# Spreading one batch's dense, transpose, gate and rank pieces over the next batch's score units

## The chip, the cores and the metric

The kernel runs on one core of one Trainium2 chip. The core's engines are TensorE (PE; its weight loads are shown apart, as PEld), VectorE (DVE), ScalarE (ACT), GpSimd (POOL) and SyncE (SP), which here only issues DMAs. Each engine works through its own list of instructions; semaphores hold an instruction back until what it needs is there. The metric is the device time of one launch in microseconds, the median of several runs.

## The reference

Two stages. The first is attention with a selection of key chunks: 4 batches, 8 heads, 768 positions, head size 64. For every query, an upper bound of its score against each 32-key chunk is computed, and the six best causal chunks are kept.

```python
k_min = np.min(k_chunks, axis=3); k_max = np.max(k_chunks, axis=3)
ub = np.sum(np.maximum(q[:, :, :, None, :] * k_min[:, :, None], q[:, :, :, None, :] * k_max[:, :, None]), axis=-1)
ub = np.where(causal, ub, -1e9)
top_chunks = np.argsort(ub, axis=-1)[..., -6:]
...                                   # mask: chunk selected and key not after query
attn = softmax(where(mask, q @ k.T / 8, -1e9));  out = attn @ v
```

The second takes the result as x, 3072 tokens of 512 numbers, through a dense two-layer network and, for each token, one of eight experts of the same form:

```python
y_dense = np.maximum(x @ w1_dense, 0) @ w2_dense
logits = x @ w_gate
expert_idx = np.argmax(logits, axis=1);  gate_w = softmax(logits)[expert_idx]
for e in range(8):
    mask = expert_idx == e
    y_moe[mask] = gate_w[mask, None] * (np.maximum(x[mask] @ w1[e], 0) @ w2[e])
return y_dense + y_moe
```

## The kernel before

Heads are worked in 16 pairs, four pairs to a batch. The scores of a pair are cut into 11 *units*: a unit is up to 512 columns of scores in one PSUM tile, one exponential on ACT, for three of the eleven a diagonal mask on POOL, and then the products with V.

```python
def scores(p, u):
    sp = psc.tile([128, 512], FP, name="sp")            # 3 PSUM buffers
    for g, kt, a, z in units[u]:
        nc.tensor.matmul(sp[:, o : o + w], kT..., rT..., ...)
    ex = aexp.tile([128, 512], HF, name="ex")
    nc.scalar.activation(ex[:, 0:o], sp[:, 0:o], AF.Exp, scale=-0.125)
    if pc[0][1] == pc[0][2]:
        latest["pool"] = nc.gpsimd.affine_select(out=ex, ...)
...
def norm(p, g):                                          # a head's rows into the batch's x tile
    nc.vector.tensor_tensor(xbig[b % 2][:, :, h0 : h0 + D], opv[:, :, 0:D], rs..., ALU.mult)
```

While batch b+1 is in attention, batch b's x goes through the second stage's first steps in small *pieces*: `xtr` (four transposes and a DVE copy), `gate` (24 small matmuls, a chain of small DVE operations), `ranks` (each token's row in a table sorted by expert), `place` (an indirect DMA, issued by POOL, that scatters 128 rows of x into that table in DRAM), and the dense network: `l1` (four matmuls, a relu on ACT) and `l2` (four matmuls, a copy on ACT, a store). In the attention part all of these share one PSUM buffer.

```python
for kind in ("tr", "h", "y", "rk"):
    cur[kind] = (pfill, "fb")                            # pfill: bufs=1
...
def xtr(mi):
    def f():
        tp = ptile("tr", [128, NK, 128], HF, "tp")
        for ko in range(NK):
            nc.tensor.transpose(tp[:, ko], xbig[b % 2][:, mi, ko * 128 : (ko + 1) * 128], ident)
        nc.vector.tensor_copy(xT[:, :, mi * 128 : (mi + 1) * 128], tp)
    return f
def gate():
    lg = ptile("tr", [128, NT, E], FP, "lg")
    ...                                                  # 24 matmuls; max, subtract, Exp, argmax, one-hot
    nc.vector.reciprocal(xbig[b % 2][:, :, Dm : Dm + 2].bitcast(FP), ss)
    nc.gpsimd.tensor_copy(xbig[b % 2][:, :, Dm + 2 : Dm + 4].bitcast(mybir.dt.int32), num[:, b * NT : (b + 1) * NT])
def l2(g, i, hold):
    def f():
        yp = ptile("y", [128, Dm], FP, "yp")
        for j in range(NK):
            nc.tensor.matmul(yp, hold["h"][:, j, i * 128 : (i + 1) * 128], wd[:, NK + j], ...)
        ys = my.tile([128, Dm], FP, name="ys")
        nc.scalar.copy(ys, yp)
        m = b * NT + g * G + i
        for j in range(NJ):
            st_ = nc.sync.dma_start(out=outv[m, j], in_=ys[64 * j : 64 * j + 64])
    return f
```

Which piece comes behind which of the next batch's 44 units is set here (NT is 6, HP*NU is 44):

```python
at = {}
for n, f in enumerate(out_list):                         # six xtr, then gate
    at.setdefault(n + n // NT, []).append(f)
at.setdefault(9, []).append(ranks)
for t in range(NT):
    at.setdefault(11 + 4 * t, []).append(place(t))
U = HP * NU
for n, f in enumerate(dense):                            # 4 l1, 3 l2, 4 l1, 3 l2
    at.setdefault(10 + n * (U - 12) // len(dense), []).append(f)
```

The source order is not the final one: a scheduler in the compiler orders each engine's instructions by readiness and priority. The second part takes the table block by block: `fetch` loads 128 rows of one expert (SyncE, into one of `eg`'s buffers), `tx` transposes them, `e1`, `th`, `e2` are the expert's two layers, and an indirect DMA adds the rows to the output. A fetch may start only when the scatters it could read have landed. The first six fetches are issued in the last pair; the last batch's own pieces go between the first blocks.

## Time and profile before

| | |
|---|---|
| time, median of 3 runs | 259.59 us (258.28 to 259.83) |
| span of the profiled execution | 256.5 us |
| granted TensorE clock over the span | 0.989 |
| HBM read, written | 41.66 MB, 18.23 MB |
| exponentials (L551), busy on ACT | 176, 92.4 us |
| score matmuls (L547), busy on PE | 384, 63.0 us |
| dense matmuls (L383, L392), busy on PE | 128 and 96, 26.2 and 24.4 us |

Line names such as L551 are lines of the kernel. "Busy" is the time in which an engine has an instruction in work; the ends of matmuls are modelled, so the spacing of starts tells more of PE's rate than durations do. "Idle before" is the time for which the engine stood before an instruction, with the one that released it behind an arrow. The page's view of the chain that ended last holds only POOL's final entry in this profile, so limits have to be read from stretches of time and from timelines.

### The profile page before, as it was taken

Reading aid. Unit: us, or ns where it says so; the run is one execution under the profiler, and the core shown is the slowest. Engines: PE = TensorE matmul, PEld = TensorE weight load, DVE = VectorE, ACT = ScalarE, POOL = GpSimd, SP = SyncE. Lnnn points to the kernel's source line nnn. Section 1 sums busy time; section 2 is a strip of 40 time slices with the busy share of each in tenths; the row PEclk is TensorE's granted clock in tenths of the full one; section 3 lists DMA queues with packets and bytes.
Section 4 is the critical chain, followed back from the end, with each engine's and each line's share of the span. In section 5 each row is a group of like instructions: output and inputs, shape, how many; then the busy total and the mean of one; then the engine's idle time right before and its main releaser. Section 6 shows DMA issues by size and latency. Waiting matters only on the chain. (4 is left out here: it accounts for less than half of the span.)

```text
span 256.5 us, 7304 instructions
## 1 busy us (share of the span) xinstructions
PE 213.9 (83%) x2547; PEld 142.2 (55%) x2547; DVE 181.2 (71%) x622; ACT 177.7 (69%) x331; POOL 161.5 (63%) x197
## 2 busy tenths in 40 slices
PE   0379787787899798899996989979999999999960
PEld 0256565575666576656664766646555555555520
DVE  6878899999968699985799997236633345455440
ACT  2689897887679888878897777964556455555430
POOL 3756988766468575867866553520787462888771
PEclk9999999999999999999999999999999999999995
DMA  7999999999749989999999894366398999688875
GB/s 181 263 265 254 209 252 235 247 224 213 199 107 225 252 204 212 202 290 171 279 230 247 140 181 125 87 169 176 98 301 133 242 277 240 113 138 107 112 105 76
DMA packets 75109, 49.89 MB, mean 195 GB/s; under 512 B 29632, under 2 KB 68160, under 8 KB 75072
## 3 DMA queue, kind: packets, MB, share of 16 engines
q1 hardware_dynamic: 59856, 30.33, 46.5%
q0 software_dynamic: 15216, 19.09, 45.4%
q8 instruction: 21, 0.34, 0.6%
q14 instruction: 16, 0.13, 0.1%
HBM read 41.66 MB, written 18.23 MB: 234 GB/s over the span
## 5 line engine op out<-in xcount | busy, mean ns | idle before, releaser
L551 ACT ACTIVATE ex<-sp 128x512 f16<-128x512 f32 (+1 forms) x176 | 92.4, 593 | 10.8 <-PE sp L547 10.6
L547 PE MATMUL sp<-rT,kT 128*128 128x128 f16 (+3 forms) x384 | 63.0, 262 | 2.4 <-ACT ex L551 0.8
L553 POOL TENSOR_SCALAR_AFFINE_SELECT ex<-ex 128x512 f16<-128x512 f16 x48 | 33.2, 699 | 37.6 <-ACT ex L551 37.5
L713 POOL DMA_INDIRECT out_dram<-yo,xg x28 | 43.7, 1561 | 20.2 <-DVE yo L712 12.1
L566 PE MATMUL op<-v,ex 128*128 128x65 f16 x672 | 48.7, 194 | 4.3 <-POOL ex L553 2.8
L566 PEld LDWEIGHTS <-ex 128*128 128x128 f16 x672 | 37.0, 98 | 17.7 <-POOL ex L553 6.2
L712 DVE TENSOR_SCALAR yo<-yp,xg 128x512 f32<-128x512 f32 x28 | 21.0, 750 | 24.9 <-PE yp L709 17.1
L368 POOL DMA_INDIRECT table<-xbig,slot x24 | 24.4, 1019 | 19.1 <-DVE nf L324 11.3
L547 PEld LDWEIGHTS <-kT 128*128 128x128 f16 x384 | 28.3, 98 | 6.7 <-issue 4.2
L703 ACT COPY ehT<-tp 128x512 f16<-128x512 f16 x28 | 16.4, 585 | 19.8 <-PE tp L701 19.8
L692 PE MATMUL hp<-we,exT 128*128 x112 | 29.1, 379 | 1.1 <-DVE xbig L577 1.1
L709 PE MATMUL yp<-we,ehT 128*128 x112 | 28.7, 379 | 0.8 <-ACT ehT L703 0.8
L383 PE MATMUL hp<-xT,wd 128*128 128x384 f16 x128 | 26.2, 325 | 1.7 <-ACT hT L385 1.1
L392 PE MATMUL yp<-wd,hT 128*128 128x512 f16 x96 | 24.4, 378 | 1.0 <-ACT ys L395 0.4
L695 ACT ACTIVATE eh<-hp 128x512 f16<-128x512 f32 x28 | 16.7, 598 | 11.5 <-PE hp L692 10.9
L395 ACT COPY ys<-yp 128x512 f32<-128x512 f32 x24 | 14.2, 593 | 10.2 <-PE yp L392 6.6
L490 DVE TENSOR_TENSOR k<-kp 128x384 f16<-128x384 f16 x32 | 13.8, 469 | 9.9 <-ACT kp L483 9.8
L385 ACT ACTIVATE hT<-hp 128x384 f16<-128x384 f32 x32 | 15.9, 496 | 6.6 <-PE hp L383 6.3
L686 DVE COPY exT<-tp 128x512 f16<-128x512 f16 x28 | 11.8, 423 | 11.5 <-PE tp L684 10.5
L483 ACT COPY kp<-pp 128x768 f16<-128x768 f16 x16 | 12.9, 804 | 7.9 <-PE pp L481 7.9
L577 DVE TENSOR_TENSOR xbig<-op,rs 128x384 f16<-128x384 f32 x32 | 17.6, 550 | 0.4
L475 POOL CAST v<-vf 128x768 f16<-128x768 f32 x16 | 13.9, 871 | 5.0 <-DMA vf<-in_v_dram 3.0
(124 smaller groups left out, 403.0 us busy)
## 6 DMA issues: line engine op xcount, KB each, us to landing
we<-in_moe_w_dram POOLq DMA_DIRECT2D x16, 512.0 KB, 8.2
kf<-in_k_dram SPq DMA_DIRECT2D x32, 192.0 KB
qf<-in_q_dram SPq DMA_DIRECT2D x32, 192.0 KB
vf<-in_v_dram SPq DMA_DIRECT2D x32, 192.0 KB
out_dram<-ys SPq DMA_DIRECT2D x48, 128.0 KB
xg<-table SPq DMA_DIRECT2D x28, 136.0 KB
table<-zt SPq DMA_DIRECT2D x9, 136.0 KB
wd<-in_moe_w_dense_dram POOLq DMA_DIRECT2D x2, 512.0 KB, 6.3
```

The source lines that it names most:

```text
L368: sc = nc.gpsimd.indirect_dma_start(out=table, out_offset=bass.IndirectOffsetOnAxis(ap=keep["slot"][:, t : t + 1], axis=0), in_=xbig[b % 2 ...
L383: nc.tensor.matmul(hp, wd[:, ko, j * 128 : (j + 1) * 128], xT[:, ko, g * G * 128 : (g + 1) * G * 128], start=(ko == 0), stop=(ko == NK - 1))
L392: nc.tensor.matmul(yp, hold["h"][:, j, i * 128 : (i + 1) * 128], wd[:, NK + j], start=(j == 0), stop=(j == NK - 1))
L547: nc.tensor.matmul(sp[:, o : o + w], kT[p % NB][g][:, kt * 128 : (kt + 1) * 128], rT[p % NB][g][:, a * 128 : z * 128], start=(o == 0), sto ...
L551: nc.scalar.activation(ex[:, 0:o], sp[:, 0:o], AF.Exp, scale=-0.125)
L553: latest["pool"] = nc.gpsimd.affine_select(out=ex, in_=ex, compare_op=ALU.is_ge, fill=0.0, base=0, pattern=[[0, 4], [1, 2], [2, 64]], chan ...
L566: nc.tensor.matmul(s["op", g][:, t * (D + 1) : (t + 1) * (D + 1)], ex[:, o : o + 128], v16[p % NB][:, g, kt, :], start=first, stop=(last_o ...
L577: nc.vector.tensor_tensor(xbig[b % 2][:, :, h0 : h0 + D], opv[:, :, 0:D], rs.to_broadcast([128, NT, D]), ALU.mult)
L692: nc.tensor.matmul(hp, s["xT"][:, ko], wef[:, bass.ds(offs[i] + ko * 512, 512)], start=(ko == 0), stop=(ko == NK - 1))
L709: nc.tensor.matmul(yp, s["hT"][:, j], wef[:, bass.ds(offs[i] + (NK + j) * 512, 512)], start=(j == 0), stop=(j == NK - 1))
L712: nc.vector.tensor_scalar(o, yp, s["x"][:, Dm : Dm + 2].bitcast(FP), None, ALU.mult)
L713: sc = nc.gpsimd.indirect_dma_start(out=out, out_offset=bass.IndirectOffsetOnAxis(ap=s["x"][:, Dm + 2 : Dm + 4].bitcast(mybir.dt.int32), a ...
```

## The change

Pieces are issued one in every two units over all of the next batch's 44 units, in one fixed order: three transposes, a dense piece, a transpose, a dense piece, two transposes, gate, ranks, and the other dense pieces. This is to keep pieces from standing close together on the shared PSUM buffer, and to keep dense matmuls from piling up late in the batch. Scatters follow the ranks three units apart. As pieces of a batch now last longer, a third x tile lets attention write ahead, and the row numbers are written into the tiles by index instructions instead of being copied after the gate. A dense piece's store is issued two units behind the piece, so that SyncE doesn't stand before it with loads behind. To make room, fetch buffers go from 14 to 12 and two key-reduction tiles from two buffers to one. The first fetches move later, since the scatters do.

```diff
-    eg = ctx.enter_context(tc.tile_pool(name="eg", bufs=14))
+    eg = ctx.enter_context(tc.tile_pool(name="eg", bufs=12))
...
-    xbig = [const.tile([128, NT, XW], HF, name=f"xbig{i}") for i in range(2)]
+    NX = 3
+    xbig = [const.tile([128, NT, XW], HF, name=f"xbig{i}") for i in range(NX)]
+    def numbers(b):
+        for j in range(NJ):
+            nc.gpsimd.iota(xbig[b % NX][64 * j : 64 * j + 64, :, Dm + 2 : Dm + 4].bitcast(mybir.dt.int32)[:, :, 0],
+                           pattern=[[128, NT]], base=b * S + j, channel_multiplier=2)
...                                    # called once for each tile at the start
-            nc.gpsimd.tensor_copy(xbig[b % 2][:, :, Dm + 2 : Dm + 4].bitcast(mybir.dt.int32), num[:, b * NT : (b + 1) * NT])
+            if b >= NX:
+                numbers(b)
...
+                hold["ys", i] = ys
+            return f
+        def store(g, i, hold):
+            def f():
+                ys = hold["ys", i]     # then the two DMAs as before
...
-        for n, f in enumerate(out_list):
-            at.setdefault(n + n // NT, []).append(f)
-        at.setdefault(9, []).append(ranks)
+        x, d = out_list[:NT], dense
+        order = x[:3] + [d[0], x[3], d[1], x[4], x[5], gate, ranks] + d[2:]
+        for n, f in enumerate(order):
+            at.setdefault(2 * n, []).append(f)
+            if f in stores:
+                at.setdefault(min(2 * n + 2, HP * NU - 2), []).append(stores[f])
         for t in range(NT):
-            at.setdefault(11 + 4 * t, []).append(place(t))
-        U = HP * NU
-        for n, f in enumerate(dense):
-            at.setdefault(10 + n * (U - 12) // len(dense), []).append(f)
+            at.setdefault(2 * order.index(ranks) + 3 + 3 * t, []).append(place(t))
...
-            k1 = ahead.tile([128, 2, NC, 16], HF, name="k1")
-            k2 = ahead.tile([128, 2, NC, 8], HF, name="k2")
+            k1 = ahead.tile([128, 2, NC, 16], HF, name="k1", bufs=1)
+            k2 = ahead.tile([128, 2, NC, 8], HF, name="k2", bufs=1)
...
-            if p == NP - 2 and u == 8:
+            if p == NP - 2 and u == NU - 1:
                 load_rows(N1)
                 load_offs()
-            if p == NP - 1 and 3 <= u < 3 + FIRST:
-                fetch(u - 3)
+            if p == NP - 1 and 4 <= u < 4 + FIRST:
+                fetch(u - 4)
...                                    # in the second part:
             extra.setdefault(1 + n * (N1 - 2) // len(d), []).append(f)
+            if f in stores:
+                extra.setdefault(2 + n * (N1 - 2) // len(d), []).append(stores[f])
```

## Prediction

> **What bounds the kernel now.** I read the table of engines first, then stretches of time, then TensorE's and the queues' timelines. Over the whole span nothing is full:
>
> ```profile
> PE 213.9 (83%) x2547; PEld 142.2 (55%) x2547; DVE 181.2 (71%) x622; ACT 177.7 (69%) x331; POOL 161.5 (63%) x197
> ```
>
> The span has two parts. Attention lasts until about 171 us: sixteen head pairs of eleven score units, whose 176 exponentials on ACT run from 16.6 to 170.7. The experts' blocks follow. I cut attention at every eleventh exponential and asked for each engine's busy time (columns: stretch, length, then PE, PEld, DVE, ACT, POOL busy, clock, DMA share, GB/s). Pairs 3, 5, 6, 7, 8, 9, 10, 13 and 14, counted from 0:
>
> ```profile
> 40.50:48.70 8.20, 6.54 (x113) 5.15 (x112) 7.95 (x32) 7.00 (x13) 5.97 (x10) 1.00 1.20 248
> ...
> 56.70:69.50 12.80, 9.96 (x156) 7.40 (x155) 12.19 (x50) 9.38 (x18) 7.30 (x9) 1.00 1.01 229
> 69.50:81.10 11.60, 10.79 (x147) 7.50 (x145) 8.72 (x31) 9.65 (x20) 8.32 (x10) 1.00 0.63 121
> 81.10:91.90 10.80, 9.13 (x117) 6.07 (x114) 8.68 (x30) 9.39 (x20) 6.43 (x9) 1.00 1.11 265
> 91.90:99.80 7.90, 6.71 (x121) 5.46 (x118) 7.63 (x28) 6.84 (x14) 5.36 (x7) 1.00 0.90 166
> 99.80:110.50 10.70, 10.02 (x161) 7.47 (x158) 10.41 (x43) 8.50 (x18) 7.16 (x9) 1.00 1.11 241
> 110.50:122.40 11.90, 10.75 (x145) 7.38 (x144) 8.58 (x33) 9.57 (x21) 9.13 (x11) 1.00 1.04 226
> ...
> 141.70:152.50 10.80, 9.54 (x160) 7.27 (x157) 10.52 (x51) 8.54 (x17) 6.35 (x8) 1.00 0.98 173
> 152.50:163.00 10.50, 10.14 (x117) 6.37 (x114) 7.16 (x33) 8.29 (x19) 4.99 (x6) 1.00 0.39 103
> ```
>
> A pair without pieces of the previous batch takes 8.2 us and DVE is busy for 7.95: DVE paces it. With pieces the limit changes hands: in pairs 5, 9 and 13 (transposes, gate, ranks) DVE holds 12.19 of 12.80, 10.41 of 10.70, 10.52 of 10.80; in 6, 10 and 14 (most of the dense pieces) PE holds 10.79 of 11.60, 10.75 of 11.90, 10.14 of 10.50, with DVE far lower. The loads are large in turn instead of together. That is what the change attacks.
>
> Where one limit hands over to the other, PE's timeline shows the pieces standing in its way:
>
> ```profile
> 61.93 0.74 PE L265 MATMUL lg<-wg,xT 128*128 128x8 f16 x24
> ...
> 64.64 0.20 PE L290 MATMUL rk<-oh,low 128*128 128x48 f16 x1 [1.19 <-DVE oh L278]
> ...
> 65.48 0.81 PE L383 MATMUL hp<-xT,wd 128*128 128x384 f16 x4
> 66.13 0.33 PE L534 MATMUL pp<-ident,fl 128*128 128x128 f16 x3
> ```
>
> The rank matmul waits 1.19 us for the gate's chain of small DVE operations, and everything behind it on PE waits too. A first-layer piece (four matmuls) holds PE from 65.48 to 66.13, 0.65 us: durations shown are longer than the spacing, so I count spacings. From 170.7 on PE alone is the limit: busy 57.54 of 58.00 us between 182 and 240, a block about every 2.2 us.
>
> The hand-over between the parts goes through DRAM. Three views, POOL's, SyncE's and PE's timelines:
>
> ```profile
> 164.48 0.97 POOL L368 DMA_INDIRECT table<-xbig,slot  x1 [0.17 <-issue]
> ```
> ```profile
> 166.94 1.44 SPq L450 DMA_DIRECT2D xg<-table  x3
> ```
> ```profile
> 171.33 0.61 PE L684 MATMUL tp<-ident,xg 128*128 128x128 f16 x8
> 173.05 1.02 PE L692 MATMUL hp<-we,exT 128*128 x4 [1.12 <-DVE xbig L577]
> ```
>
> The last scatter of batch 2 into the table starts at 164.48; the first fetch of a block, which must wait for its landing, starts 2.46 us later; its rows are read at 171.33, directly after the last attention matmul, without a wait. So there are some two microseconds to spare.
>
> **What the Trainium skill says.** "Perfetto Trace Analysis", section "Optimization Strategy", says that where the most-contended engine changes over time, interleaving the regimes may help. The stretches above are this case. "PSUM — Partial Sum Buffer", section "Engine vs sequencer instructions", says that matmuls start and complete in program order and the queues of ScalarE, VectorE and GpSimdE are strictly first in, first out; the 1.19 us wait at 64.64, with nothing of PE started in it, agrees. "TensorE: Matmul & The Clock Gate", section "Back-to-back issue gap", gives N/2.4 + 2.5 ns for one warm matmul, 162.5 ns at N=384; the trace has 0.65/4 = 162 ns. "DMA: Bandwidth & Descriptors", section "Two DMAs through the same engine are not ordered", says only a completion semaphore orders a write and a later read; hence the 2.46 us above.
>
> **The change part by part.**
>
> Work per batch stays the same. From spacings: eight first-layer pieces 8 x 0.65 = 5.2 us of PE, six second-layer ones (71.04 to 71.90) 6 x 0.86 = 5.2, six transposes at 0.22 = 1.3, gate 0.6, ranks 0.4: 12.7 us. On DVE six copies of 0.414 = 2.5, gate and ranks about 1.9 more (62.71 to 65.6, without what lies between). On ACT 14 evictions spaced some 0.4 to 0.5, about 6.2.
>
> *Spacing.* Before, six transposes come in units 0 to 5, gate in 7, ranks in 9, dense pieces from 10 to 39. After, transposes, two dense pieces, gate and ranks fill units 0 to 18 and dense pieces go to 42. In the compiled order of PE's instructions I added up what stands between score matmuls, by spacing (0.0285 us for a 65-column one, 0.056 for a transpose): the heaviest pair of each batch carries 10.0, 9.7, 9.8 us before and 7.2, 7.0, 6.0 after; adding 2.24 us of scores (5376 columns at 2.4 per ns) gives 12.2 against 9.4. The longest run without a score matmul falls from 3.5, 2.3, 3.3 to 3.5, 1.6, 1.25: batch 0 keeps its bunch.
>
> After, by units: 0 to 10 are paced by DVE, 7.7 (mean of pairs 1 to 4) + 4 x 0.42 = 9.4. Units 11 to 21 too: 7.7 + 0.8 + 1.9 = 10.4. Then ACT decides, with 6.75 of its own (eleven exponentials at the spacing of 0.485 and two copies of 0.7): 6.75 + 6 pieces x 0.44 = 9.4, and 6.75 + 5 x 0.44 = 9.0. Sum 38.2 a batch. The same sum before, largest engine of each pair: 12.2 + 10.8 + 9.4 + 7.6 = 40.0 in batch 0, and 10.4 + 10.75 + 9.0 + 9.3 = 39.5 in batch 1. All pairs from 56.7 on sum to 106.8 in 114.0 us, so a microsecond of limit costs 1.07. Gain 1.8 + 1.3 in the first two, times 1.07 = 3.3. In batch 2 the last two pairs prepare no further head, so work put off to them was cheap already, and the lists of blocks (about 2.5 us of DVE) now fall a pair later: I count 0.4. Together 3.7.
>
> *Waits of the pieces.* All pieces share one PSUM buffer. PE idle just before transposes is 3.2 us and before ranks 2.1 us between 48.7 and 170.7. A piece two units later finds the buffer free and the gate done. Some of this is already in the 6% above the sum of limits; I count a quarter of the 5.3: 1.3.
>
> *Third x tile, row numbers.* The copy of the row numbers after the gate once held POOL for 2.5 us until scatters had landed; index writes made once replace it. POOL is not the limit there: 0. Four more index writes of 0.15 to 0.36 us at 35.6 lie on a POOL that is 80% busy: 0. The single buffers for the key reduction are written and read by DVE alone: 0.
>
> *Stores queued behind.* SyncE waits 21 us for evictions in attention, and loads stand behind; but POOL's waits for k, q and v in pieces' time are nil. Worth 0.
>
> *Hand-over.* Scatters of batch 2 move from units 11 to 31 to units 21 to 36, so the last stands behind pair 15's last diagonal mask. That mask ends at 168.62 in the old time base: scatter 168.8, landed and first fetch 171.2, data about 1.9 us after that (its packets in the old trace end at 168.5 to 169.2) = 173.1, second block 173.6. The old reads were at 171.33 and the matmul at 173.05 after a DVE wait that will be over by then. New first expert matmul about 174.2: +1.2 lost. One dense piece of 0.86 us now lies in that hole, already counted in the work.
>
> *Expert part.* The 28 blocks are the same; 12 fetch buffers instead of 14 make fetch i wait for scatter i-12. Fetch 12 ran at 197.3, scatter 0 at 182.5 with 5.1 to land: free. The last dense stores come a block later in the source, but in SyncE's compiled order stand behind the same scatter 7: 0.
>
> Sum: -3.7 - 1.3 + 1.2 = -3.8, so 259.6 - 3.8 = 255.8 us.
>
> **Rivals.** *Hand-over dominates.* If attention gets no faster and the late scatter costs 2.5 us: 262. For it: the landing chain is serial and PE reads in order; against it: that attention has idle on every engine. *DVE stays the limit.* DVE's total is unchanged, 92 us of 114 from 56.7 on; it was busy 95% in pairs without pieces, and if the old overload was already absorbed by preparing two pairs ahead, evening out gives nothing: about 259 to 260. *Full evening-out.* DVE and ACT each total some 93; if they are kept 88% busy, attention shrinks by 8 and with the lost 1.2 the time is 253. For it: the three gaps of 4.5 to 5.4 us between exponentials that end at 69.5, 110.5 and 152.5; against it: batch 0 keeps its bunch, and three engines loaded alike wait for each other more.
>
> **Range and chances.** Between the rivals' 253 and 262, with a little beyond: 251.5 to 260.8. Faster by over 2% means below 254.4, that is 5.2 us against the 3.8 worked out: 0.32. Slower by over 2% is above 264.8 and needs more than the whole hand-over loss: 0.05. The rest, 0.63, is within.
>
> **What would show it.** Right: in stretches of eleven exponentials no pair above about 11 us from pair 5 on, DVE no longer over 11 in one; PE's idle before transposes and ranks below 1.5 us together; the last exponential about 5 us earlier; scatter-to-fetch chain ending after attention with PE idle 1 to 2 us before its first block transpose; expert part as long as before. Wrong: the last exponential at the old place, the hole at the hand-over above 3 us, or PE idle in the expert part from late fetches.

## The result, and the profile after

The changed kernel takes 266.26 us (median of 4 runs, 265.66 to 266.54) against 259.33 for the kernel before on the same chip: a ratio of 1.027 [1.023 to 1.031]. It is slower, by almost twice as much as the prediction said it would be faster. The page of the kernel after begins:

```profile
PE 216.7 (82%) x2547; PEld 143.0 (54%) x2547; DVE 186.5 (71%) x622; ACT 178.4 (68%) x331; POOL 161.5 (61%) x200
```

PE and DVE run exactly as many instructions as before and are busy longer: PE by 2.8 us, DVE by 5.3. POOL has three instructions more and the same busy time.

To see where the time went I cut both traces at the same events: every eleventh exponential, the first transposes of the third block (the first of a block that nothing holds up), and the end. "Hand-over" is from the last exponential to that third block, "experts" the rest.

| us | to pair 1 | pairs 1–4 | pairs 5–8 | pairs 9–12 | pairs 13–15 | hand-over | experts | span |
|---|---|---|---|---|---|---|---|---|
| before | 24.3 | 32.4 | 43.2 | 41.8 | 29.0 | 7.5 | 78.3 | 256.5 |
| after | 23.9 | 36.0 | 41.1 | 42.4 | 29.4 | 9.9 | 81.7 | 264.3 |
| difference | -0.4 | **+3.6** | -2.1 | +0.6 | +0.4 | **+2.4** | **+3.4** | +7.8 |

The profiled execution of before is its fastest one (258.28), so the differences sum to 0.9 more than the medians do. Three stages lose. Of the 3.6 us in pairs 1 to 4, pairs 1 to 3 lose 2.1 us (26.5 after, 24.4 before). Pair 4 loses 1.5 (9.43 us; 7.95 before), but there the cut itself moves: after, ACT makes the next pair's q tile ahead of the first exponential of pair 5, before it made it behind. The kernel with the new spacing alone, further below, has 9.37 us in pair 4 as well. So pair 4 belongs to the spacing, and pairs 4 to 8 together take 50.6 us instead of 51.1: batch 0 gains about 0.6 us and not 2.1.

*Pairs with pieces.* Busy time in stretches of the kernel after, for pairs 6, 7, 10 and 11 (columns as in the prediction):

```profile
68.90:80.00 11.10, 10.08 (x153) 7.12 (x150) 9.43 (x40) 8.84 (x20) 8.18 (x10) 1.00 0.74 173
80.00:92.00 12.00, 10.86 (x136) 7.35 (x135) 9.49 (x35) 9.96 (x21) 8.51 (x10) 1.00 0.99 237
...
110.70:123.40 12.70, 11.03 (x156) 7.43 (x156) 11.55 (x41) 9.54 (x20) 9.34 (x11) 1.00 1.03 199
123.40:135.40 12.00, 10.36 (x139) 7.17 (x139) 10.16 (x36) 9.47 (x20) 9.35 (x11) 1.00 1.03 257
```

Pairs 5 and 9 are shorter, as intended (9.0 and 9.6 us; 12.9 and 10.7 before), but the load moved into the two pairs behind each. Counted by the matmuls in PE's timeline, the 14 dense pieces of batch 0 lie about 2, 4, 7 and 1 in pairs 5 to 8 (8, 17, 27 and 4 matmuls), where the prediction counted 2, 1, 6 and 5: even spacing in the source did not come out even. In the stretch from 110.70, PE holds 11.03 us and DVE 11.55 of 12.70: both are near their limit. In the waits of PE between 48.7 and 170.7 us (waits in total, how many, the longest) the pieces' own waits went away, and others came:

```profile
PE pp L533 <- DVE kb L507: 4.7, 5, 1.2
PE sp L560 <- ACT ex L564: 2.5, 6, 0.7
...
PE rk L295 <- DVE oh L282: 1.3, 2, 0.7
...
PE tp L261 <- DVE xbig L590: 0.3, 1, 0.3
```

The same view of the kernel before had:

```profile
PE tp L257 <- DVE xT L258: 2.7, 3, 1.0
PE rk L290 <- DVE oh L278: 2.1, 3, 1.2
...
PE pp L520 <- DVE kb L494: 0.7, 2, 0.5
```

Transposes no longer wait for the copies that free their buffer; ranks still wait 1.3 us. But PE now stands 4.7 us before the chunk scores until DVE has the reduced keys (kb), against 0.7, and 2.5 us before scores until an exponential has freed a buffer.

*Pairs 1 to 4.* Why are the reduced keys late? DVE's timeline after shows the two halving steps of the key reduction (max and min of two halves; x2 is both of them):

```profile
39.21 1.75 DVE L503 TENSOR_TENSOR k<-kp 128x384 f16<-128x384 f16 x2
40.88 2.44 DVE L504 TENSOR_TENSOR k<-k 128x192 f16<-128x192 f16 x2
```

The same two lines before, at nearly the same place:

```profile
40.62 0.65 DVE L490 TENSOR_TENSOR k<-kp 128x384 f16<-128x384 f16 x2
41.19 0.88 DVE L491 TENSOR_TENSOR k<-k 128x192 f16<-128x192 f16 x2
```

1.53 us became 4.19. The work of these lines is the same; what differs is POOL's timeline at that time, here after:

```profile
39.78 0.96 POOL L481 CAST k<-kf 128x768 f16<-128x768 f32 x1
40.69 0.95 POOL L483 CAST q<-qf 128x768 f16<-128x768 f32 x1
41.60 0.66 POOL L566 TENSOR_SCALAR_AFFINE_SELECT ex<-ex 128x512 f16<-128x512 f16 x1
42.22 0.81 POOL L488 CAST v<-vf 128x768 f16<-128x768 f32 x1
```

The four POOL instructions stand without a gap from 39.78 to 43.03, and the second step gets through only about when they end; its first half takes 2271 ns, where the shortest of the 32 takes 243 ns. POOL's set-up block in pair 2 (tiles filled, constants, row numbers) takes 3.8 us instead of 2.7: three tile fills and six index writes instead of two fills and two index writes. So, counted from the start of pair 1, the k cast comes 1.1 us later than before. The key reduction comes 1.05 us earlier, as a DVE copy ahead of it takes 0.39 us instead of 1.45, which before lay beside two masks on POOL. Before, the casts ran from 39.03 to 40.79 and were all but over when the key reduction began. Over the whole kernel the 32 first steps take 582 ns in the mean instead of 469, or 3.6 us more in sum, and the second steps 452 instead of 405, or 1.5 more: nearly all that DVE's busy time grew by.

The Trainium skill, "SBUF — State Buffer", section "SBUF: two separate sides", describes this: VectorE and GpSimd share one pair of SBUF ports as an exclusive lock, taken by a VectorE operation in a two-port mode or, against a GpSimd operation that reads SBUF, by one with two SBUF inputs; the loser "fully blocks". The trace agrees: the step that took 2271 ns has two SBUF inputs and lies under casts and a mask that read SBUF. The prediction did not use it.

*Hand-over.* The last scatter (POOL), the first fetch (SyncE's queue), the first read and the first expert matmul (PE) of the kernel after:

```profile
171.30 0.98 POOL L373 DMA_INDIRECT table<-xbig,slot  x1 [0.17 <-issue]
```
```profile
173.80 3.38 SPq L463 DMA_DIRECT2D xg<-table  x6
```
```profile
176.06 0.40 PE L700 MATMUL tp<-ident,xg 128*128 128x128 f16 x4 [0.94 <-DMA xg<-table]
...
177.50 0.81 PE L708 MATMUL hp<-we,exT 128*128 x3 [0.46 <-DVE exT L702]
```

The chain of scatter, landing, fetch and read is the same as before, but begins only 1.4 us ahead of the last exponential (172.7) instead of 6.2. From the last exponential to the first expert matmul it is now 4.8 us, before 2.4.

*Experts.* From the tenth to the eleventh block after takes 6.5 us, before 3.9. ACT's copies of dense results into store buffers show it, after:

```profile
208.10 0.59 ACT L400 COPY ys<-yp 128x512 f32<-128x512 f32 x1 [2.25 <-DMA out_dram<-ys]
210.40 0.59 ACT L400 COPY ys<-yp 128x512 f32<-128x512 f32 x1 [1.72 <-DMA out_dram<-ys]
```

They wait for earlier stores to land, since there are three such buffers, and PE's second expert layer waits 1.63 us for ACT at 208.74.

In SyncE's queue the stores of dense results that wait there went out ahead of the next two fetches before, and go out behind two (from 200.88) after. Before, then after:

```profile
195.32 1.12 SPq L398 DMA_DIRECT2D out_dram<-ys  x2
```
```profile
201.95 1.12 SPq L409 DMA_DIRECT2D out_dram<-ys  x2
```

Counted from the tenth block (200.5 and 205.0), the store begins 5.2 us ahead of it before, and 3.1 after.

### The profile page after: what moved, and what is told of

Its sections match the earlier page's. It is cut to its first block, busy times and chain, and to the rows that moved or that the text cites. A ratio compares the mean times of both kernels' runs of the same rounds, so it can differ in the third digit from the quotient of the medians.

```text
span 264.3 us, 7322 instructions
## 1 busy us (share of the span) xinstructions
PE 216.7 (82%) x2547; PEld 143.0 (54%) x2547; DVE 186.5 (71%) x622; ACT 178.4 (68%) x331; POOL 161.5 (61%) x200
## 5 line engine op out<-in xcount | busy, mean ns | idle before, releaser
L560 PE MATMUL sp<-rT,kT 128*128 128x128 f16 (+3 forms) x384 | 65.4, 265 | 4.0 <-ACT ex L564 2.9
L579 PE MATMUL op<-v,ex 128*128 128x65 f16 x672 | 49.3, 195 | 3.2 <-POOL ex L566 2.1
L579 PEld LDWEIGHTS <-ex 128*128 128x128 f16 x672 | 37.7, 99 | 15.8 <-POOL ex L566 6.0
L373 POOL DMA_INDIRECT table<-xbig,slot x24 | 24.3, 1012 | 20.2 <-DVE nf L329 12.5
L560 PEld LDWEIGHTS <-kT 128*128 128x128 f16 x384 | 29.1, 99 | 9.2 <-issue 6.3
L388 PE MATMUL hp<-xT,wd 128*128 128x384 f16 x128 | 26.2, 325 | 0.8 <-ACT ys L400 0.3
L397 PE MATMUL yp<-wd,hT 128*128 128x512 f16 x96 | 24.3, 378 | 1.6 <-ACT ys L400 1.0
L711 ACT ACTIVATE eh<-hp 128x512 f16<-128x512 f32 x28 | 16.7, 597 | 11.3 <-PE hp L708 11.3
L503 DVE TENSOR_TENSOR k<-kp 128x384 f16<-128x384 f16 x32 | 17.3, 582 | 7.3 <-ACT kp L496 7.3
L400 ACT COPY ys<-yp 128x512 f32<-128x512 f32 x24 | 14.3, 596 | 11.5 <-PE yp L397 6.3
L533 PE MATMUL pp<-kb,qp 128*128 128x48 f16 x192 | 11.1, 185 | 11.3 <-DVE kb L507 11.2
```

Of the source, the lines that this page charges most:

```text
L373: sc = nc.gpsimd.indirect_dma_start(out=table, out_offset=bass.IndirectOffsetOnAxis(ap=keep["slot"][:, t : t + 1], axis=0), in_=xbig[b % N ...
L388: nc.tensor.matmul(hp, wd[:, ko, j * 128 : (j + 1) * 128], xT[:, ko, g * G * 128 : (g + 1) * G * 128], start=(ko == 0), stop=(ko == NK - 1))
L560: nc.tensor.matmul(sp[:, o : o + w], kT[p % NB][g][:, kt * 128 : (kt + 1) * 128], rT[p % NB][g][:, a * 128 : z * 128], start=(o == 0), sto ...
L579: nc.tensor.matmul(s["op", g][:, t * (D + 1) : (t + 1) * (D + 1)], ex[:, o : o + 128], v16[p % NB][:, g, kt, :], start=first, stop=(last_o ...
```

## The experiments

Each ratio is to the kernel before in the same session on the same chip. The kernel before itself took 258.2 to 264.3 us in six sessions on different chips, so absolute times are compared only within a chip. The stages are from one profiled execution of each.

### One part of the change undone

Stores issued with their pieces again, in the expert part, where it matters:

```diff
-                extra.setdefault(2 + n * (N1 - 2) // len(d), []).append(stores[f])
+                extra.setdefault(1 + n * (N1 - 2) // len(d), []).append(stores[f])
```

> The changed kernel with one edit: in the expert part the last batch's dense stores are issued with their piece again, not one block later. SyncE's order changes in 8 rows, no other engine's order changes. Ledger theory: between the 9th and 15th block transposes the changed kernel lost 3.2 us against the kernel before because its three store buffers were freed late (ACT's copies stood 2.25, 1.72 and 0.90 us for stores to land); so 266.3 - 3 = 263.3 us, with ACT's wait for stores down to about 2 us. Rival: the expert part was late only because it started late, and PE would have stalled on scatters anyway: no change, 265.5 to 266.5.

Row numbers made once and copied after the gate, as before, with three tiles (two long index writes and three copies in pair 2, instead of six index writes):

```diff
-            numbers(b)
...
+        for j in range(NJ):
+            nc.gpsimd.iota(num[64 * j : 64 * j + 64, :, 0], pattern=[[128, NM]], base=j, channel_multiplier=2)
...
-            if b >= NX:
-                numbers(b)
+            nc.gpsimd.tensor_copy(xbig[b % NX][:, :, Dm + 2 : Dm + 4].bitcast(mybir.dt.int32), num[:, b * NT : (b + 1) * NT])
```

> The changed kernel with one edit: row numbers again written once into a table of their own and copied by POOL after the gate, as in the kernel before. Only POOL's order changes. Theory of collisions: POOL's longer block of set-up instructions in pair 2 moved its k and q casts by 0.75 us under DVE's two fp16 key-reduction lines, which then took 1.2 and 2.1 us too long in pair 3; pairs 2 to 4 should go back from 9.1, 9.7, 9.4 to about 8.5, 8.2, 8.0 us and the time to about 263.3. Rival: the single buffers of the key reduction (kept here) make DVE slower: pairs 2 to 4 stay above 9 and the time at 266.

Scatters two units apart instead of three, fetches one unit earlier:

```diff
-            at.setdefault(2 * order.index(ranks) + 3 + 3 * t, []).append(place(t))
+            at.setdefault(2 * order.index(ranks) + 2 + 2 * t, []).append(place(t))
...
-            if p == NP - 1 and 4 <= u < 4 + FIRST:
-                fetch(u - 4)
+            if p == NP - 1 and 3 <= u < 3 + FIRST:
+                fetch(u - 3)
```

> The changed kernel with one edit: the six scatters of a batch follow the ranks two units apart, from unit 20 to unit 30, instead of three apart from 21 to 36, and the first six fetches one unit earlier, so that the last scatter stands where it did in the kernel before. Theory: PE's first block transpose waits for the chain last scatter, landing, fetch, landing (171.3, 173.8, 176.1); with the scatters back it comes within 1 us of the last exponential instead of 3.4, and the time is 266.3 - 2.4 = 263.9. Rival: the fetches stand behind dense stores on SyncE's queue, which haven't moved, so the gap stays above 2.5 us and the time above 265.5.

And all three together:

> The three edits together: what is left of the change is the new spacing of pieces, the third x tile, the fewer buffers and stores two units behind in attention. If the three losses are separate and add up: 266.3 - 3 - 3 - 2.4 = 257.9 us, a little under the kernel before (259.3). Rival, that the spacing itself costs time and the three are symptoms: above 260.

| | ratio to before | pairs 1–4 | pairs 5–8 | pairs 9–12 | hand-over | experts |
|---|---|---|---|---|---|---|
| stores at once | 1.0129 [1.0053, 1.0204] | 35.9 | 41.8 | 42.6 | 10.1 | 80.4 |
| numbers copied | 1.0104 [1.0031, 1.0176] | 34.4 | 41.9 | 42.5 | 9.9 | 81.6 |
| scatters earlier | 1.0077 [1.0051, 1.0104] | 34.0 | 42.9 | 42.3 | 8.3 | 80.8 |
| all three | 1.0051 [1.0026, 1.0076] | 34.3 | 41.7 | 42.3 | 8.3 | 81.0 |

Each ratio is lower than the changed kernel's, which was 1.027 above and is 1.021 in the repeat below. But the changed kernel was not run on this chip, and the first two intervals overlap the repeat's, 1.0123 to 1.0301; only the last two lie clear below it. Nor can the experts column be set against the first table: two kernels further below, whose expert part is that of the kernel before, take 82.3 and 82.5 us there on their chips. All three edits together leave half a per cent of loss. Earlier scatters bring the hand-over from 9.9 to 8.3 us, as they should; but 2.0 us of what this kernel shows is not theirs. It lies in pairs 1 to 4, where no scatter is due and where the compiled order of PE, DVE, ACT and POOL is that of the changed kernel. DVE's second halving step and the mask on POOL, in this run:

```profile
41.05 1.04 DVE L504 TENSOR_TENSOR k<-k 128x192 f16<-128x192 f16 x2
```
```profile
41.87 0.74 POOL L566 TENSOR_SCALAR_AFFINE_SELECT ex<-ex 128x512 f16<-128x512 f16 x1
```

The q cast ends at 41.81 and the mask, whose exponential is some 0.2 us later here, starts at 41.87: in that gap DVE gets in, and the step takes 1.04 us instead of 2.44. In the changed kernel the mask followed the cast without a gap. Pairs 5 to 8, 1.8 us longer here, give most of it back. How often either happens in the timed runs isn't known, so the ratio of this kernel is not to be read to the last tenth, and the 1.6 us that copied numbers win in the same pairs can't be told from it. What the three undone leave is the spacing together with the third tile and its fill, fewer buffers, and the late stores in attention. Pairs 1 to 4 are still 1.9 us longer than in the kernel before, and there is no gain.

### A repeat, and the casts moved

The changed kernel once more on another chip, then both kernels, and the three undone, with the k and q casts issued three units later:

```diff
-            if u == 7:
+            if u == 10:
                 with tc.issue_after(latest["pool"].ins):
                     cast_qk(p + 3)
```

> The changed kernel itself, so that the next ones have it on the same chip. Expected 1.027 of the kernel before, as measured first; the single-edit runs so far (1.013, 1.010, 1.008 on another chip, where the kernel before took 263.3) cannot be read without it.

> The changed kernel with POOL's k and q casts (and the loads behind them) asked for three units later in a pair, at unit 10 instead of 7, so that they no longer run beside DVE's fp16 key reduction. The same work. Collision theory: DVE's SBUF-to-SBUF fp16 lines take 21.2 us longer in sum than their shortest form in the changed kernel, 17.0 in the kernel before; here under 13, the key-reduction lines near 0.31 and 0.21 us, attention 4 us shorter than in the changed kernel on the same chip. Rival: DVE is busy but not what pairs wait for, or the stretch comes back under other POOL work: attention within 1 us of the changed kernel's.

> The kernel before with the same move of the casts. Collision theory: its 17.0 us of stretch fall too, to about 11, and it gets 2 to 3 us faster (ratio about 0.99). Rival: no difference, because the kernel before already had its casts beside other DVE work in most pairs (ratio 1.00), or slower where casts come too late for the transposes.

> The changed kernel with scatters earlier, stores at once in the expert part, row numbers copied, and the casts moved. If the losses of the change are collisions, the hand-over and the late stores, nothing but the spacing is left, and it should beat the kernel before: ratio 0.98 to 0.99. Rival: spacing itself gains nothing: ratio 1.00 or above, no better than the kernel before with moved casts.

The repeat gave 1.0212 [1.0123, 1.0301], with 35.9 us in pairs 1 to 4, 9.7 in the hand-over and 80.3 in the experts: attention and the hand-over come out alike on both chips, the experts 1.4 us apart. Later casts made no version faster: after 1.031 [1.0225, 1.0396], before 1.0126 [1.0034, 1.0218], the three undone 1.0112 [1.0084, 1.014]. In the changed kernel the two key-reduction steps do get shorter, 427 and 342 ns in the mean against 544 and 471 in the repeat. But the casts then stretch other DVE lines: a copy of the queries takes 623 ns instead of 465, one of the keys 510 instead of 399. Pair 1 takes 10.11 us, 7.76 without the move. At this place the collision was moved, not shed; other places were not tried. (The expectations put the undisturbed steps at 0.31 and 0.21 us; the shortest in the traces are 0.34 and 0.24.)

### The collision by itself

To the kernel before, five index writes of a spare tile that nobody reads, in the set-up block:

```diff
+    spare = const.tile([128, 6], mybir.dt.int32)
...
+        for _ in range(5):
+            nc.gpsimd.iota(spare, pattern=[[1, 6]], base=0, channel_multiplier=2)
```

> The kernel before with five idle index writes of POOL added to its set-up block in pair 2 (about 0.75 us of POOL's time, read by nobody); no other engine's order changes. If the changed kernel lost its 3.6 us between pairs 1 and 5 because POOL's casts and masks slid under DVE's fp16 lines, the same slide alone should do it here: pairs 2 to 4 from 8.5, 8.2, 8.0 to above 9 in one or two of them, attention and total 1.5 to 3.5 us longer (ratio 1.006 to 1.013). Rival: POOL has slack there (80% busy) and 0.75 us vanishes: ratio 1.00, pairs as before.

It gave 1.0107 [1.0061, 1.0152]: 0.7 us of idle work on POOL costs some 2.8 us of the kernel. Pairs 1 to 4 take 34.7 us instead of 32.4, and DVE's timeline shows where:

```profile
39.10 3.60 DVE L493 TENSOR_TENSOR k<-kp 128x384 f16<-128x384 f16 x2
```

The line took 0.65 in the kernel before. Counted from the start of pair 1, POOL's casts start 0.6 us later than there, but DVE, whose copy of 1.45 us takes 0.36 here, arrives 1.0 us earlier, and stands under POOL's casts, copies and mask in a row. So a small shift can turn one collision into a worse one.

The second experiment takes one of the two SBUF inputs of the first step away: it reads one half of the keys from PSUM, where the transposes left them. This pairs keys of different chunks, so these three kernels compute other chunk maxima than the reference and choose other chunks; the amount of work stays.

```diff
-                nc.vector.tensor_tensor(k1[:, i], kc[:, :, 0:16], kc[:, :, 16:32], op)
+                nc.vector.tensor_tensor(k1[:, i].rearrange("d (T c) w -> d T c w", c=4),
+                                        pk.rearrange("d (T j c w) -> d T j c w", j=NJ, c=4, w=16)[:, :, 0],
+                                        kp.rearrange("d (T c w j) -> d T c w j", j=NJ, c=4, w=16)[:, :, :, :, 1], op)
```

> The changed kernel with the first key-reduction line reading one of its two operands from PSUM instead of SBUF, the pairs of keys chosen accordingly; same result, same count of instructions, the compiler's order shifts somewhat. Collision theory: these lines took from 0.31 to 1.8 us, 18.6 us in sum; reading PSUM they should all take the same, about 0.45 us, 14.5 in sum, whatever POOL does; attention 2 to 4 us shorter than in the changed kernel. Rival: they stretch as before (then POOL's work is not what stretches them), or they don't and attention is no shorter.

> The kernel before with the same line read from PSUM. It loses 5.0 us of stretch in these lines but each is 0.14 us longer, 4.5 us in sum: no gain expected, ratio 0.995 to 1.005, where the changed kernel gains. Rival: gain as large as in the changed kernel, so that collisions do not tell the two apart.

> The changed kernel with earlier scatters, stores at once and copied row numbers, and the key line read from PSUM: collisions on that line, the hand-over and the late stores are all gone. If these made up the loss: ratio 0.985 to 0.995. If the spacing is worth nothing even so: 1.00.

Ratios: after 1.0291 [1.0227, 1.0356], before 1.0167 [1.0103, 1.0231], the three undone 1.0251 [1.0207, 1.0296]. DVE's groups by shape, in the kernel before with this edit (count, busy us, mean ns):

```profile
L490 DVE TENSOR_TENSOR k<-pp,kp 128x384 f16<-128x384 f16 x32 | 16.6, 550 | 9.3 <-ACT kp L483 9.2
L493 DVE TENSOR_TENSOR k<-k 128x192 f16<-128x192 f16 x32 | 16.3, 538 | 0.0
```

and in the kernel before itself:

```profile
L490 DVE TENSOR_TENSOR k<-kp 128x384 f16<-128x384 f16 x32 | 13.8, 469 | 9.9 <-ACT kp L483 9.8
L491 DVE TENSOR_TENSOR k<-k 128x192 f16<-128x192 f16 x32 | 11.8, 405 | 0.0
```

With a PSUM operand all 32 instances take 535 to 558 ns, whatever POOL does; with both operands in SBUF they took 335 to 997 ns before and 339 to 1795 after. So on this line the stretch goes with the second SBUF input, which fits the condition in the skill's section. As a remedy it fails: the two-SBUF form takes 335 ns at its shortest, and the step behind it, which still reads SBUF twice, now collects the stretch (405 to 538 ns in the mean). So does a copy of the queries in pair 1, 2.22 us instead of 0.75, and that pair takes 11.3 us instead of 7.8.

### One part alone, on the kernel before

The kernel before against itself, as a measure of the comparison:

> The kernel before itself, to have its profile on the chip of the next three: ratio 1.00; pairs 1 to 4 in 32.4 us, pairs 5 to 8 in 43.2, 9 to 12 in 41.8, from pair 13 to the last exponential 29.0, from there to the third block transpose 7.5.

0.9998 [0.997, 1.0026]. The stores one step later than their pieces:

```diff
                 dense.append(l2(g, i, hold))
+                stores[dense[-1]] = store(g, i, hold)
...
             extra.setdefault(1 + n * (N1 - 2) // len(d), []).append(f)
+            if f in stores:
+                extra.setdefault(2 + n * (N1 - 2) // len(d), []).append(stores[f])
```

> The kernel before with one part of the change alone: in the expert part the dense stores come one block later. SyncE's order differs in 8 rows, nothing else. Theory: late stores free the three store buffers late, ACT and then PE stand; the stretch from the third block transpose to the end grows by 2 to 3 us over the kernel before on the same chip, ratio 1.008 to 1.012. Rival: the stall in the changed kernel needs its fewer fetch buffers (12 for 14), which aren't in here: no change.

1.0024 [1.0002, 1.0046]. Its profiled execution has 81.0 us in the experts, against 77.8 in the repeat of before, 5.9 us between the tenth and the eleventh block, and the same wait for a store to land, 1.75 us on ACT. But this execution took 260.71 us, and the median is 259.34 (258.40 to 261.05), so the trace shows the effect at its largest. Alone it is worth 0.6 us in the median. Nor do late stores always cost these blocks time: with scatters earlier, or numbers copied, the stores are as late as in the changed kernel, and from the tenth to the eleventh block it is 3.9 and 4.35 us.

The scatters later, so that the last falls into unit 36 as in the changed kernel, but with the two x tiles of before:

```diff
-            at.setdefault(11 + 4 * t, []).append(place(t))
+            at.setdefault(11 + 5 * t, []).append(place(t))
...
-            if p == NP - 1 and 3 <= u < 3 + FIRST:
-                fetch(u - 3)
+            if p == NP - 1 and 4 <= u < 4 + FIRST:
+                fetch(u - 4)
```

> The kernel before with the scatters five units apart, so that the last one stands at unit 36 as in the changed kernel, and the first fetches one unit later. Theory: the chain scatter, landing, fetch, landing ends after attention; from the last exponential to the third block transpose 9.5 to 10 us instead of 7.5, ratio 1.006 to 1.01. Rival: hidden behind the last batch's own start: below 8 us, ratio 1.00.

1.034 [1.0306, 1.0373], far beyond what was expected. The hand-over takes 11.5 us instead of 7.5, with pairs 13 to 15 as long as before (29.0). The rest lies in two pairs: pair 8 takes 11.25 us instead of 7.97 and pair 12 13.96 instead of 9.56. POOL's timeline gives the cause:

```profile
94.63 0.19 POOL L282 COPY xbig<-num 128x6 int32<-128x6 int32 x1 [4.06 <-DMA table<-xbig,slot]
...
140.19 0.19 POOL L282 COPY xbig<-num 128x6 int32<-128x6 int32 x1 [6.06 <-DMA table<-xbig,slot]
```

and PE's what it costs:

```profile
141.05 0.40 PE L566 MATMUL op<-v,ex 128*128 128x65 f16 x4 [4.67 <-POOL ex L553]
```

With two tiles batch 2 writes into the tile of batch 0, so the copy of its row numbers must wait until the last scatter of batch 0 has read it, and the compiler has put that copy only a few instructions behind the scatter; POOL stands in order behind that copy, the next mask comes late, and PE waits 2.67 us for it in pair 8 and 4.67 in pair 12. The changed kernel, with three tiles, has as late scatters and not this loss: there one index write, that of batch 3, waits 3.0 us, at 94.23, and PE waits for no mask beside it. No run changes the number of tiles alone.

Only the new order and spacing of the pieces, with scatters two units apart, without the third tile, the index writes or the late stores:

```diff
-        for n, f in enumerate(out_list):
-            at.setdefault(n + n // NT, []).append(f)
-        at.setdefault(9, []).append(ranks)
+        x, d = out_list[:NT], dense
+        order = x[:3] + [d[0], x[3], d[1], x[4], x[5], out_list[NT], ranks] + d[2:]
+        for n, f in enumerate(order):
+            at.setdefault(2 * n, []).append(f)
...
-            at.setdefault(11 + 4 * t, []).append(place(t))
+            at.setdefault(2 * order.index(ranks) + 2 + 2 * t, []).append(place(t))
...
```

> The kernel before with the new order and spacing of pieces alone: two x tiles, 14 fetch buffers, stores at once, copied row numbers, two buffers each in the key reduction, last scatter at unit 30. If even loads are worth what the prediction said: pairs 5 to the last exponential 3 to 4 us shorter than in the kernel before, ratio 0.985. What the runs so far suggest: pairs 5 to 8 about 1.5 us shorter, pairs 9 to 12 and the rest up to 1 us longer, 0 to 1 us in all, ratio 0.995 to 1.003.

1.0004 [0.9979, 1.0029]: nothing. Against the repeat of before, pairs 5 to 8 take 41.2 us instead of 43.2, but pair 4 takes 9.37 instead of 8.34, and pairs 9 to 12 take 43.8 instead of 41.8. What batch 0 gains, batch 1 gives back, mainly in pairs 10 and 11, which are 12.78 and 11.91 us long here as in the changed kernel (11.87 and 9.76 before). The profiled execution took 261.37 us, the longest of twelve with a median of 258.93, so its stages sum to 2.4 us too much.

### The set-up block out of the way

At the start POOL waits 2.66 us for the first keys. The last pair of runs puts the whole set-up block there, in both kernels; only the filler store to the table stays in pair 2:

```diff
+        route_consts()
         cast_qk(0)
...
                     with tc.issue_after(st[n2]["cast"].ins):
-                        route_consts()
+                        nc.sync.dma_start(out=table[EMPTY : EMPTY + 128], in_=zt)
```

> The kernel before with its block of set-up work on GpSimd (tiles filled, row numbers, constants) moved out of pair 2 into the 2.66 us in which GpSimd waits for the first keys; the filler store to the table stays where it is. If GpSimd's work as such only costs where it lies beside VectorE's copies and key reductions, pair 2 and pair 3 lose nothing and may gain up to 1 us (the fold's copy of 1450 ns at 37.9 goes back to 362): ratio 0.995 to 1.0. The rival, that every shift of GpSimd's casts only moves the stretch to other lines: VectorE's sum in pairs 1 to 4 as large as before, ratio 1.0 within its interval. A third: the first fills delay the first casts or share VectorE's port during its own fills, and the start grows by up to 1 us: ratio 1.004.

> The changed kernel with the same block (now with three fills and six index writes) in the wait for the first keys. If what pairs 1 to 4 lose against the kernel before (36.0 against 32.4 us) comes from the longer block in pair 2 and the phase of the casts that it sets, the stretch falls to 32 to 33.5 us, the key reductions at 39 to 41 us take 0.4 to 0.9 us instead of 1.75 to 2.44, and the ratio to before falls from 1.021-1.027 to 1.008-1.015 (the late scatters and stores stay). The rival, that the spacing of the pieces or the single key-reduction buffers cost those pairs: they stay above 35 us, ratio 1.02 or more.

| us | to pair 1 | pair 1 | pairs 2–4 | pairs 9–12 | ratio to before |
|---|---|---|---|---|---|
| before | 24.3 | 7.8 | 24.6 | 41.8 | 1 |
| before, block early | 24.5 | 7.8 | 23.8 | 43.8 | 1.0032 [0.9996, 1.0069] |
| after | 23.9 | 7.8 | 28.2 | 42.4 | 1.021 to 1.027 |
| after, block early | 26.2 | 9.7 | 24.8 | 42.5 | 1.0225 [1.0179, 1.0271] |

In the changed kernel pairs 2 to 4 fall from 28.2 to 24.8 us, the level of the kernel before. DVE's timeline has the fourth and the fifth key reduction; the fifth is the one that took 4.19 us:

```profile
34.54 1.28 DVE L502 TENSOR_TENSOR k<-kp 128x384 f16<-128x384 f16 x2
35.74 1.04 DVE L503 TENSOR_TENSOR k<-k 128x192 f16<-128x192 f16 x2
...
43.91 0.63 DVE L502 TENSOR_TENSOR k<-kp 128x384 f16<-128x384 f16 x2
44.46 0.88 DVE L503 TENSOR_TENSOR k<-k 128x192 f16<-128x192 f16 x2
```

The fifth takes 1.51 us in place of 4.19. That settles the cause in these pairs: the block, not the single buffers of the key reduction, which this kernel still has. But pairs 1 to 4 take 34.5 us where 32 to 33.5 were expected, and the total hardly moves. The longer block ends after the first keys have come, so the first cast begins at 6.00 us, the first key reduction stands under casts (2.67 us for its first step at 8.56), and the first exponential comes at 18.1 us instead of 16.3. In pair 1 POOL stands 2.5 us before a weight load, for a cause that the profile doesn't show; its masks come late, PE waits 1.4 us for one, and the casts now lie over the fourth key reduction, which takes 2.32 us instead of 1.50. The start and pair 1 lose somewhat more than pairs 2 to 4 gain. In the kernel before, 0.8 us won in pairs 2 to 4 comes back as a longer pair 10 (13.25 us against 11.86). No version ran faster than the kernel before beyond its interval.

## Why the prediction was wrong

**The bounds and the limits of single pairs** were read rightly: pairs 5, 9 and 13 were DVE's, the dense ones PE's.

**Spacing, predicted 3.7 us gained: measured nothing when alone. This is the largest miss.** For batch 0 the sum of limits seems to hold: pairs 5 to 8 were to shrink by 1.9 us and shrank by 2.1 in the changed kernel. That is luck. Pair 5 came out at 9.0 us and pair 7 at 12.0, where the prediction's limits times 1.07 give 10.1 for both, and with pair 4 the gain is 0.6. For batch 1 it was to be 1.4 and was a loss of 0.6. (The largest engines from 56.7 us on sum to 107.8, not 106.8, and the factor is 1.06; the gain of 3.3 stays.) The step that failed is the sum of "the largest engine of each pair" times 1.07. It gave the units from 22 to 32, which fall mainly into pairs 7 and 11, to ACT with 9.4 us; these pairs took 12.0, with PE at 10.86 and 10.36, DVE at 9.49 and 10.16 and ACT at 9.96 and 9.47. Pair 10, DVE's by the prediction with 10.4, took 12.8 with DVE at 11.55, of which part is the stretched key reduction. Two things went into it. The dense pieces did not spread as counted, 4 and 7 of them in pairs 6 and 7 instead of 1 and 6. And where one engine towers over the others a pair is about as long as that engine's work, but where three are nearly equal it is longer than any of them. The kernel before showed that already: its pair 7, with 9.13, 8.68 and 9.39 us of PE, DVE and ACT, took 10.80. The spacing alone gave a time close to the 259 to 260 us of the rival "DVE stays the limit"; whether for the rival's reason isn't shown.

**Waits of the pieces, predicted 1.3 gained: they went away and others took their place.** Transposes and ranks waited 4.8 us together in the lines above and wait 1.6 now, close to the mark set; PE's waits for the reduced keys rose by 4.0 and for exponentials to 2.5. Here a wait that went away at one instruction came back at another.

**"Four more index writes ... lie on a POOL that is 80% busy: 0": measured +2.1 us in pairs 1 to 3.** The step that failed is that work on an engine with slack costs nothing. (80% is the mean of pairs 1 to 4; in pair 2, where the block lies, POOL was busy for 7.58 of 8.40 us.) The index writes and the third fill are cheap themselves. They shift the casts behind them, and those block DVE's two-input key reduction. Two experiments show it: idle index writes added to the kernel before cost 1.07%, and with the block elsewhere pairs 2 to 4 are as long as before. The 1.6 us that copied numbers won fit, but the kernel with earlier scatters won 2.0 in the same pairs without such an edit. That DVE's busy time in a pair without pieces was 95% was in the prediction, and so was POOL's load; that the two shut each other out was not. The single key-reduction buffers show no cost, but no run tests them alone.

**Stores queued behind, predicted 0 in attention:** no run tests the attention part alone. **Expert part, "the last dense stores come a block later ... : 0":** the trace has +3.4 us. The order in SyncE's queue was looked at, but not that the store buffers, three of them, would come free later and hold ACT and then PE. Its size is the least settled: late stores alone cost 0.6 us in the median, the stage takes 81.6 and 80.8 us with late stores on one chip, 81.0 and 80.4 with prompt ones, and on another it differs by 1.3 to 2.5. The rest of the 3.4 stays open.

**Hand-over, predicted 1.2 lost: mechanism right, 2.4 lost.** From the last exponential to the first read of a block it is 3.3 us, where the prediction's chain gives 2.4. The scatter starts 1.4 us ahead of the last exponential and not 1.9, the fetch comes 2.5 us after it as foreseen, and the data needs 2.3 us and not 1.9. Scatters brought forward win back 1.6 of the 2.4, and later ones on the kernel before lose 4.0 there; why 1.6 more than here stays open.

**Third tile: no cost of its own was predicted.** The late scatters need it, as far as the runs tell: late scatters on two tiles cost 7.2 us in pairs 5 to 12.

Undoing the stores, the numbers and the scatters brings 1.021 to 1.027 down to 1.005, on another chip. The sum of the prediction was thus wrong in two ways: the gain was not there, and three items set down as 0, 0 and 1.2 cost most of what was lost. Of the signs named for being wrong, the hole at the hand-over is above 3 us, and the last exponential came not at the old place but 2.1 us later.

## What to carry to other kernels

Before adding even small GpSimd work to a stretch where VectorE sets the pace, look at which VectorE lines with two SBUF operands stand beside GpSimd's instructions: the busy shares say nothing of it, but the spread of durations of one line at one shape does. Evening out loads helps less as the engines become equal: the sum of the largest engines is then a floor and not an estimate. When a store, scatter or fill is moved later, ask for the buffer that it frees and for the in-order queue that stands behind that buffer.

## What the hardware showed that was not expected

- A DVE instruction with two SBUF inputs can be held through several POOL instructions in a row, not only one: 2271 ns for a step of 243 ns at its shortest, under a cast, a mask and another cast standing without a gap. POOL lost little in return: its 48 casts took 0.85 us in the mean in both kernels, 0.81 to 1.10 each.
- The same line with one operand in PSUM took 535 to 558 ns in all 32 instances.
- In one pair of traces it got in when POOL left a gap: with 0.06 us between two POOL instructions the two second steps took 1.04 us instead of 2.44, in a stretch with the same order of instructions on PE, DVE, ACT and POOL.
- The kernel before took 258.2 us on one chip and 264.3 on another, 2.3% apart, with the executions on one chip within 0.6 to 2.1%.
